# Fourier mix with its features folded a second time, and low parts made in pieces of 256 columns

## The chip, the cores and the metric

The kernel runs on one core of a Trainium2 chip. The time is in device microseconds (us), from the start of the program's execution to its end; lower is better. The engines are PE (matrix products; PEld is its weight loads), DVE, ACT and POOL (elementwise work) and SP (issues most transfers). Each engine executes its own instructions in a fixed order. About 0.3% (2 us) is what a measurement of this kernel can tell from no change.

## The reference

Local and global attention is followed by two mixer blocks on two sequences of 768 tokens with 512 features. The change lies in the second block:

```python
def _moe2_ref(x, w_ch1, w_ch2):
    X = np.fft.fft(x, axis=1)
    X = np.fft.fft(X, axis=2)
    mixed = np.real(X).astype(np.float32)
    u = x + mixed
    mu = np.mean(u, axis=-1, keepdims=True)
    var = np.mean((u - mu) ** 2, axis=-1, keepdims=True)
    un = (u - mu) / np.sqrt(var + 1e-06)
    ch = np.maximum(un @ w_ch1, 0.0) @ w_ch2
    return (u + ch).astype(np.float32)
```

The real part of the two transforms is cos-cos minus sin-sin: tokens times a 768-point table, then features times a 512-point table.

## The kernel before, in words

**Precision.** Products take float32r operands, which keep part of a float32. So each operand is split into a high part (a cast) and a low part (the rest), and a product is three matmuls: high by high, high by low, low by high.

**The main work** is `ffn`: 64 chunks c, each with a word of weights of 128x1024 (512 columns of the first matrix, 512 of the second). Chunk c needs its word c cast to `wh` by ACT (L196), the low part `wo` made by POOL (L200), 12 matmuls of 512 columns (L225; the last four read `wo`), `gh` by ACT (L232) and `gl` by DVE (L233), and 12 matmuls (L248) one chunk later. Chunks 0 to 47 are the first block for three groups of 512 tokens, 48 to 63 the second for one group. The other two groups go through `unit` (L1009, L1059) at the end. Words 0 to 15 are decoded on DVE (L166, L169, L171) as they come in; later ones are read back from a scratch in DRAM.

**The side work** comes in generators that `drive` steps between the main work's steps, at a rate given per stretch of 64 steps: transposes (`tr_gen`), `fft_tables` (loads the cos and sin tables on POOL's DMA queue), `fft(0)`, `norm`, `fft(1)`, `unit_tokens`. Within an engine a scheduler then orders the instructions, so some stand earlier or later than in the code; the rows below headed by an engine show the order that comes out.

**`fft(b)`** for a sequence: `fold` adds and subtracts token tiles, then columns 1 to 255 and 511 to 257 of the features, so the cosine half needs 257 columns and the sine half 255. It makes high and low parts `ee`, `oo` (and `em` for the middle token). First stage: products with tables `c1`, `s1` (L824, L848) give `pt` and `qt`. Second stage: `pcos` (six matmuls L861 of 258 columns, one with `sgn`, L863) and six of 256 columns (L874) for each of three token tiles, and one `pcos` more. ACT and DVE add the results into `x` (L877 to L884).

Of the kernel before, what the change touches and what calls it, by code (L numbers as in the profile page):

```python
# [20 lines left out]
NF = FF // P  # L21
# [3 lines left out]
NL_MAX = 97  # L25
J1 = 386
K1 = 258
JP, KP = 416, 288
KW = S + (NT - 1) * P
PRE_LOAD = (0, 1, 3, 4)  # L30
PRE_DECODE = (2, 3, 4, 6)
# [8 lines left out]
class Prog:  # L40
# [147 lines left out]
    def w_split(self, c):  # L188
        if c >= PLAIN:
            return  # L190
        nc = self.nc
        raw = self.w32.pop(c)
        hi = self.wp.tile([P, 2 * D], FR, tag="whi", bufs=3, name=f"wh{c}")
        lo = self.wp.tile([P, 2 * D], FR, tag="wlo", bufs=3, name=f"wo{c}")
        keep = self.tc.keep_in_program_order if c == 0 else lambda i: i
        keep(nc.scalar.copy(hi, raw))  # L196

        n = 2 * D // (4 if c < NF else 2)
        for z in range(0, 2 * D, n):
            keep(nc.gpsimd.tensor_tensor(lo[:, z:z + n], raw[:, z:z + n], hi[:, z:z + n].bitcast(F32), ALU.subtract))  # L200
        self.wq[c] = (hi, lo)
# [519 lines left out]
    def fft_open(self, ctx):  # L721
        nc, a, tc = self.nc, self.a, self.tc
        self.fp = ctx.enter_context(tc.tile_pool(name="fft", bufs=1))
        fp = self.fp
        self.ct = {}
        shapes = [(f"{n}{z}", shape, w) for n, shape, w in (("c1", [3, JP], J1), ("s1", [3, 384], 384), ("c2", [2, KP], K1),
                                                            ("s2", [2, 256], 256)) for z in range(2)]
        shapes += [("alt", [JP], J1)]

        for n, shape, w in shapes:  # L730
            t = fp.tile([P] + shape, FR, name=n)
            self.ct[n] = t[:, :, 0:w] if len(shape) == 2 else t[:, 0:w]

    def fft_tables(self):
        nc, a, ct = self.nc, self.a, self.ct
        for n in ("c1", "s1", "c2", "s2"):
            for z in range(2):
                nc.gpsimd.dma_start(ct[f"{n}{z}"], a[f"{n}{z}"][:, :, 0:256] if n == "s2" else a[f"{n}{z}"])
                yield
        nc.gpsimd.memset(ct["alt"][64:128, :].bitcast(F32), 0.0)  # L740
        nc.gpsimd.dma_start(ct["alt"][0:64, :], a["alt"])
        yield
        nc.vector.memset(self.mh, -0.5)
# [8 lines left out]
    def fft(self, b):  # L752
        nc, fp, ct = self.nc, self.fp, self.ct
        A = [self.x[b * NT + i] for i in range(3)]
        Bp = [self.x[b * NT + 3 + i] for i in range(3)]
        xm = self.dist[1][:, 0:D]
        nc.gpsimd.memset(xm, 0.0)
        for z in range(2):
            nc.gpsimd.memset(self.dist[z][:, 3 * K1 - 2:3 * K1], 0.0)
        for r in (0, 32):  # L760
            nc.sync.dma_start(xm[r:r + 1, :], Bp[0][0:1, :])
        yield
        ee = fp.tile([P, 2, 3, KP], FR, tag="ee", bufs=1, name=f"ee{b}")[:, :, :, 0:K1]
        oo = fp.tile([P, 2, 3, 256], FR, tag="oo", bufs=1, name=f"oo{b}")
        ee, oo = [ee[:, z] for z in range(2)], [oo[:, z] for z in range(2)]

        def fold(rows, E, O, h, l, i):
            if O is False:
                f = self.qkb[i % 2][:, 1024:1024 + K1]
                nc.vector.tensor_tensor(f[0:rows, 1:256], E[:, 1:256], E[:, 511:256:-1], ALU.add)  # L770
                nc.vector.tensor_copy(f[0:rows, 0:257:256], E[:, 0:257:256])
                nc.vector.memset(f[0:rows, 257:258], 0.0)
            else:
                f = self.vb[i % 2][:, 1024:1024 + K1]
                nc.vector.tensor_tensor(f[0:rows, 1:256], E[:, 1:256], E[:, 511:256:-1], ALU.subtract)
                nc.vector.memset(f[0:rows, 0:1], 0.0)
            n = K1 if O is False else 256
            nc.scalar.copy(h, f[0:rows, 0:n])
            if l is None:
                f, l = f[32:33], h[32:33]  # L780
                nc.vector.tensor_tensor(l, f[:, 0:n], l.bitcast(F32), ALU.subtract)
            else:
                nc.vector.tensor_tensor(l, f[0:rows, 0:n], h.bitcast(F32), ALU.subtract)

        em = fp.tile([P, KP], FR, tag="em", bufs=1, name=f"em{b}")[:, 0:K1]
        for i in range(3):
            E, O = (self.qkb[z][:, (i % 2) * D:(i % 2 + 1) * D] for z in range(2))
            nc.vector.tensor_tensor(E, A[i], Bp[i], ALU.add)
            fold(P, E, False, ee[0][:, i, :], ee[1][:, i, :], i)
            yield  # L790
            nc.vector.tensor_tensor(O, A[i], Bp[i], ALU.subtract)
            fold(P, O, True, oo[0][:, i, :], oo[1][:, i, :], i)
            if i == 1:
                fold(P, xm, False, em, None, 0)
            yield
        if b == 1:
            for _ in range(6):
# [42 lines left out]
        qt = fp.tile([P, 2, 2, 384], FR, tag="ee", bufs=1, name=f"fqt{b}")  # L840
        qt = [qt[:, z] for z in range(2)]
        for dd in range(2):
            cs = slice(dd * P, (dd + 1) * P)
            pp = self.psum("m")
            n = 0
# [6 lines left out]
            h, l = qt[0][:, dd, :], qt[1][:, dd, :]  # L852
# [1 line left out]
            nc.vector.tensor_tensor(l, pp[:, 0:384], h.bitcast(F32), ALU.subtract)  # L854
            yield

        def pcos(out, at):
            n = 0
            for dd in range(2):
                for x, y in PS:  # L860
                    nc.tensor.matmul(out, lhsT=at(pt[x][:, dd, :]), rhs=c2[y][:, dd, :], start=n == 0, stop=False)  # L861
                    n += 1
            nc.tensor.matmul(out, lhsT=at(pr), rhs=ct["sgn"], start=False, stop=True)  # L863

        for i in range(3):
            js = slice(i * P, (i + 1) * P)
            pc = self.psum("m")
            pcos(pc[:, 0:K1], lambda m: m[:, js])
            yield
            qs = self.psum("m2")  # L870
            n = 0
            for dd in range(2):
                for x, y in PS:
                    nc.tensor.matmul(qs[:, 0:256], lhsT=qt[x][:, dd, js], rhs=s2[y][:, dd, :], start=n == 0, stop=n == 5)  # L874
                    n += 1
            qc = self.dist[i % 2][:, 2 * K1:3 * K1]
            nc.scalar.copy(qc[:, 0:256], qs[:, 0:256])  # L877
            sm = self.dist[0][:, 0:K1]
            dm = self.dist[0][:, K1:2 * K1]
            nc.vector.tensor_tensor(dm, pc[:, 0:K1], qc, ALU.subtract)  # L880
            nc.vector.tensor_tensor(sm, pc[:, 0:K1], qc, ALU.add)
            for X, lo_, hi_ in ((A[i], dm, sm), (Bp[i], sm, dm)):
                nc.vector.tensor_tensor(X[:, 0:257], X[:, 0:257], lo_[:, 0:257], ALU.add)
                nc.vector.tensor_tensor(X[:, 511:256:-1], X[:, 511:256:-1], hi_[:, 1:256], ALU.add)  # L884
            yield
        pc = self.psum("m")
        pcos(pc[:, 0:K1], lambda m: same(m[:, 384:385]))
        X = Bp[0]
        nc.vector.tensor_tensor(X[0:1, 0:257], pc[0:1, 0:257], xm[0:1, 0:257], ALU.add)
        nc.vector.tensor_tensor(X[0:1, 511:256:-1], pc[0:1, 1:256], xm[0:1, 511:256:-1], ALU.add)  # L890
        yield

    def norm_one(self, i, z):
# [198 lines left out]


def arm(tc, pg, fast):
# [204 lines left out]
```

## Time and profile before

| | us |
|---|---|
| median of 3 runs | 662.1 |
| runs | 660.75 to 662.32 |
| the profiled execution | 660.77 |
| its span, first to last instruction | 658.4 |
| PE busy | 643.9 |
| DVE busy | 425.1 |
| POOL busy | 344.6 |
| ACT busy | 298.0 |

Busy PE counts overlapping matmuls, so it isn't PE at its peak. How long a matmul really holds PE is the distance from its start to the start of the next one. The mean granted clock of TensorE over the span is 0.995 of full speed.

### The profile page before, as it was taken

The page shows a single profiled execution, that of the slowest core. Times are in us where ns is not written, and L with a number is a line of the kernel's source. Part 1 is how long each engine was busy: PE and PEld are TensorE (multiplying, and loading weights), DVE is VectorE, ACT ScalarE, POOL GpSimd, SP SyncE. Part 2 cuts the span into 40 slices and gives each one's busy share as a digit, 9 for nine tenths or more (in the row PEclk, how much of TensorE's full clock was granted, in tenths as well). Part 3 has the DMA queues.
Part 4 walks back from the last instruction along what each step waited for, and adds up shares of the span by engine and source line. Part 5 has one row for each costly group of instructions (what it writes and reads, how often), then busy time and mean ns, then how long its engine had stood idle before and what let it go on. Part 6 is the DMA issues. An engine that isn't in the chain of part 4 may idle for free.

```text
span 658.4 us, 9572 instructions
## 1 busy us (share of the span) xinstructions
PE 643.9 (98%) x3442; PEld 534.5 (81%) x3442; DVE 425.1 (65%) x784; ACT 298.0 (45%) x584; POOL 344.6 (52%) x360
## 2 busy tenths in 40 slices
PE   7998999999999999999999999999999999999996
PEld 6877777888888888888888888888888888888885
DVE  5889778897839434387467765387556545464544
ACT  5887874554344434335334433334543443233430
POOL 4130235787986554566347665165484664446610
PEclk8999999999999999999999999999999999999998
DMA  7678806888995967666463962112011111011003
GB/s 256 222 275 288 293 35 200 243 246 270 309 335 185 318 216 252 232 199 220 164 208 114 314 226 66 63 65 96 33 67 62 65 64 65 9 56 64 2 2 132
DMA packets 33866, 107.51 MB, mean 163 GB/s; under 512 B 3920, under 2 KB 7952, under 8 KB 30736
## 3 DMA queue, kind: packets, MB, share of 16 engines
q1 hardware_dynamic: 31104, 102.23, 45.8%
q0 software_dynamic: 2416, 3.65, 2.1%
q10 hardware_dynamic: 288, 0.92, 0.4%
q8 instruction: 29, 0.48, 0.3%
q14 instruction: 29, 0.24, 0.1%
HBM read 86.75 MB, written 20.02 MB: 162 GB/s over the span
## 4 chain that ended last, share of the span: by engine, by line
PE 89%; DVE 7%; ACT 2%; issue 1%; DMA 0%; DVEq 0%; ACTq 0%
PE ps_h L225 27%; PE ps_acc L248 27%; PE ps_acc L1059 13%; PE ps_h L1009 10%; DVE p L559 3%; PE ps_sd L1009 2%; DVE pt L591 1%; PE ps_sd L605 1%; PE ps_sd L297 1%; PE ps_sd L824 1%; PE ps_sd L848 1%; PE ps_acc L537 1%; ACT p L571 1%; PE ps_sd L580 1%; PE ps_sd L861 1%
## 5 line engine op out<-in xcount | busy, mean ns | idle before, releaser
L200 POOL TENSOR_TENSOR wo<-w,wh 128x512 fp32r<-128x512 f32 (+1 forms) x160 | 206.6, 1316 | 134.8 <-ACT wh L196 123.4
L225 PE MATMUL ps_h<-uT,wh 128*128 128x512 f32 x512 | 131.5, 393 | 0.0
L196 ACT CAST wh<-w 128x1024 fp32r<-128x1024 f32 x64 | 67.4, 1054 | 101.4 <-PE ps_acc L248 55.5
L225 PEld LDWEIGHTS ps_h<-uT,wh 128*128 128x128 f32 x512 | 94.4, 188 | 19.3 <-issue 0.8
L248 PE MATMUL ps_acc<-wh,gh 128*128 128x512 f32 x256 | 101.0, 395 | 0.0
L248 PE MATMUL ps_acc<-wh,gl 128*128 128x512 f32 x256 | 100.0, 391 | 0.0
L248 PE MATMUL ps_acc<-wo,gh 128*128 128x512 f32 x256 | 99.7, 390 | 0.0
L233 DVE SCALAR_TENSOR_TENSOR gl<-ps_h,gh 128x512 fp32r<-128x512 f32 x64 | 43.8, 684 | 74.0 <-ACT gh L232 74.0
L990 POOL TENSOR_TENSOR uo<-ur,uh 128x256 fp32r<-128x256 f32 (+1 forms) x40 | 42.2, 1065 | 59.6 <-ACT uh L987 59.6
L232 ACT ACTIVATE gh<-ps_h 128x512 fp32r<-128x512 f32 x64 | 38.3, 598 | 70.1 <-PE ps_h L225 70.1
L225 PE MATMUL ps_h<-uT,wo 128*128 128x512 f32 x256 | 69.0, 390 | 0.0
L248 PEld LDWEIGHTS ps_acc<-wh,gl 128*128 128x128 f32 x256 | 48.0, 188 | 10.6 <-DVE gl L233 0.3
L1065 DVE TENSOR_TENSOR xall<-ps_acc,xall 128x512 f32<-128x512 f32 x56 | 38.2, 691 | 28.2 <-PE ps_acc L1059 28.2
L225 PEld LDWEIGHTS ps_h<-uT,wo 128*128 128x128 f32 x256 | 48.0, 188 | 10.3
L248 PEld LDWEIGHTS ps_acc<-wo,gh 128*128 128x128 f32 x256 | 48.1, 188 | 9.6 <-issue 0.2
L248 PEld LDWEIGHTS ps_acc<-wh,gh 128*128 128x128 f32 x256 | 48.1, 188 | 9.4 <-issue 0.2
L571 ACT ACTIVATE p<-p,m 128x256 f32<-128x256 f32 (+2 forms) x96 | 47.6, 499 | 8.7 <-DVE m L559 8.6
L169 DVE SCALAR_TENSOR_TENSOR wr<-wr 128x1024 int32<-128x1024 int32 x30 | 44.1, 1470 | 10.7 <-ACT wr L164 9.5
L987 ACT CAST uh<-ur 128x256 fp32r<-128x256 f32 (+1 forms) x40 | 18.8, 488 | 68.7 <-PE ps_acc L1059 62.9
L1009 PE MATMUL ps_h<-op,uh 128*128 128x512 f32 x160 | 49.3, 389 | 0.0
L559 DVE CUSTOM_DVE_ANT_0 p<-ps_acc,dist 128x256 f32<-128x256 f32 (+2 forms) x96 | 34.9, 419 | 7.4 <-PE ps_acc L542 6.8
L1009 PEld LDWEIGHTS ps_h<-op,uh 128*128 128x128 f32 x160 | 30.0, 188 | 6.3
(268 smaller groups left out, 1142.6 us busy)
## 6 DMA issues: line engine op xcount, KB each, us to landing
w<-wscr SPq DMA_DIRECT2D x48, 512.0 KB, 4.2
wr<-wl SPq DMA_DIRECT2D x17, 1024.0 KB, 7.8
wr<-wl SPq DMA_DIRECT2D x60, 256.0 KB, 5.4
wscr<-w SPq DMA_DIRECT2D x16, 512.0 KB, 8.4
wscr<-wd SPq DMA_DIRECT2D x16, 512.0 KB, 3.0
ur<-wscr SPq DMA_DIRECT2D x16, 512.0 KB, 4.5
qk<-qkg SPq DMA_DIRECT2D x7, 1088.0 KB, 7.7
vb<-vw SPq DMA_DIRECT2D x7, 768.0 KB, 5.1
```

The costliest lines, as they stand in the source:

```text
L169: pin(nc.vector.scalar_tensor_tensor(lo, hi, 3, lo, ALU.logical_shift_left, ALU.bitwise_or))
L196: keep(nc.scalar.copy(hi, raw))
L200: keep(nc.gpsimd.tensor_tensor(lo[:, z:z + n], raw[:, z:z + n], hi[:, z:z + n].bitcast(F32), ALU.subtract))
L225: nc.tensor.matmul(hp, lhsT=w[:, dd * P:(dd + 1) * P], rhs=u[:, dd, :], start=n == 0, stop=n == 11)
L232: nc.scalar.activation(gh, hp, AF.Relu)
L233: nc.vector.scalar_tensor_tensor(gl, hp, 0.0, gh.bitcast(F32), ALU.max, ALU.subtract)
L248: nc.tensor.matmul(acc[t], lhsT=g[:, s], rhs=w[:, D:2 * D], start=pf == 0 and m == 0, stop=pf == NF - 1 and m == 2)
L559: keep(nc.vector.tensor_tensor_reduce(out=T[z][:, s], in0=sp[z][:, s], in1=self.dist[z][:, dcol[t]:dcol[t] + width[t]], op0=ALU.add, op1=A ...
L571: keep(nc.scalar.activation(T[z][:, s], T[z][:, s], AF.Exp, bias=m[:, z, y:y + 1], scale=-1.0, accum_out=sm[:, u % 2, y, z:z + 1]))
L990: nc.gpsimd.tensor_tensor(lo[:, s], src, hi[:, s].bitcast(F32), ALU.subtract)
L1009: keep(nc.tensor.matmul(out, lhsT=x[:, s], rhs=y[:, kt, :], start=start and kt + n == 0, stop=kt + n == 3, skip_group_check=not start))
L1059: keep(nc.tensor.matmul(acc[t], lhsT=x[:, s], rhs=y[:, w], start=first and n == 0, stop=not first and n == 2))
```

## The change

It does four things. The folded features are folded once more (128 and 129 columns), which parts the second stage's outputs into even and odd columns: each product then has the first or the second half of the contraction and 130 columns, where both halves had 258 or 256. The tables `c2` and `s2` are therefore loaded raw (`c2r`, `s2r`) and every second column of them is copied by ACT into the tables in use. Results are interleaved again as they are read. `w_split` makes `wo` in four pieces of 256 columns for all words; before, words 16 to 63 had two of 512. The last stretch's side rate goes from 1.33 to 1.42.

```diff
@@ w_split
-        n = 2 * D // (4 if c < NF else 2)
+        n = 2 * D // 4
@@ fft_tables
+        for n in ("c2", "s2"):
+            raw = []
+            for z in range(2):
+                r, src, row = self.fp.tile([P, KP], FR, tag=f"r{z}", bufs=1, name=f"{n}r{z}")[:, 0:K1], a[f"{n}{z}"], int(n == "s2")
+                raw.append(r)
+                nc.gpsimd.dma_start(r[row:P, :], src[row:P, 0, :])
+                if row:
+                    nc.gpsimd.dma_start(r[0:1, :], src[0:1, 1, :])
+            yield
+            for z in range(2):
+                t, r = ct[f"{n}{z}"], raw[z]
+                nc.vector.memset(t[:, :, KH - 1:KH].bitcast(F32), 0.0)
+                for y in range(2):
+                    nc.scalar.copy(t[:, y, 0:KH - 1], r[:, y:K1:2])
                 yield
@@ fold
             if O is False:
-                f = self.qkb[i % 2][:, 1024:1024 + K1]
-                nc.vector.tensor_tensor(f[0:rows, 1:256], E[:, 1:256], E[:, 511:256:-1], ALU.add)
-                nc.vector.tensor_copy(f[0:rows, 0:257:256], E[:, 0:257:256])
-                nc.vector.memset(f[0:rows, 257:258], 0.0)
+                f, g = (self.qkb[i % 2][0:rows, o:o + 257] for o in (1024, 1312))
+                nc.vector.tensor_tensor(f[:, 1:256], E[0:rows, 1:256], E[0:rows, 511:256:-1], ALU.add)
+                nc.scalar.copy(f[:, 0:257:256], E[0:rows, 0:257:256])
+                nc.vector.tensor_tensor(g[:, 0:128], f[:, 0:128], f[:, 256:128:-1], ALU.add)
+                nc.vector.tensor_tensor(g[:, 128:256], f[:, 0:128], f[:, 256:128:-1], ALU.subtract)
+                nc.scalar.copy(g[:, 256:257], f[:, 128:129])
             else:
...
+                nc.vector.tensor_tensor(g[:, 0:128], f[:, 0:128], f[:, 256:128:-1], ALU.subtract)
+                nc.vector.tensor_tensor(g[:, 128:256], f[:, 0:128], f[:, 256:128:-1], ALU.add)
+                nc.scalar.copy(g[:, 128:129], f[:, 128:129])
@@ second stage
-        def pcos(out, at):
-            n = 0
-            for dd in range(2):
-                for x, y in PS:
-                    nc.tensor.matmul(out, lhsT=at(pt[x][:, dd, :]), rhs=c2[y][:, dd, :], start=n == 0, stop=False)
-                    n += 1
-            nc.tensor.matmul(out, lhsT=at(pr), rhs=ct["sgn"], start=False, stop=True)
+        def pcos(pc, at):
+            for t, out in enumerate(halves(pc)):
+                for n, (x, y) in enumerate(PS):
+                    nc.tensor.matmul(out, lhsT=at(pt[x][:, t, :]), rhs=c2[y][:, t, :], start=n == 0, stop=t == 1 and n == 2)
+                if t == 0:
+                    nc.tensor.matmul(out, lhsT=at(pr), rhs=ct["sgn"][:, 0:KH], start=False, stop=True)
...
@@ arm
-                              pg.unit_tokens()), 1.33)
+                              pg.unit_tokens()), 1.42)
```

**ACT at the table loads.** Names carry their word or chunk: `wh16` is the high part of word 16, `gh15` the output of chunk 15; `c2r0` is the raw cosine table, `DMASW` a transfer on POOL's queue. Before, ACT's order there is:

```order
L196 CAST wh15_2115<-w15_2080 128x1024 [waits DVE_49,PE_49]
L232 ACTIVATE gh14_2137<-ps_h_2124 128x512 [waits PE_49,Activation_49]
L196 CAST wh16_2153<-w16_2122 128x1024 [waits DMAHW0_49,PE_49,Pool_49]
L232 ACTIVATE gh15_2173<-ps_h_2160 128x512 [waits DVE_49,PE_49]
L196 CAST wh17_2203<-w17_2158 128x1024 [waits DMAHW2_49,PE_49,Pool_49]
L232 ACTIVATE gh16_2226<-ps_h_2212 128x512 [waits DVE_49,PE_49]
```

and now:

```order
L232 ACTIVATE gh14_2137<-ps_h_2124 128x512 [waits PE_49,Activation_49]
L754 COPY c20_2200<-c2r0_2589 128x129 [waits DMASW4_49]
L754 COPY c20_2200<-c2r0_2589 128x129
L754 COPY c21_2201<-c2r1_2591 128x129 [waits DMASW5_49]
L196 CAST wh16_2153<-w16_2122 128x1024 [waits DMAHW0_49,PE_49,Pool_49]
L754 COPY c21_2201<-c2r1_2591 128x129
L232 ACTIVATE gh15_2175<-ps_h_2162 128x512 [waits DVE_49,PE_49]
L754 COPY s20_2202<-s2r0_2711 128x129 [waits DMASW2_49,DMASW1_49]
L754 COPY s20_2202<-s2r0_2711 128x129
L754 COPY s21_2203<-s2r1_2714 128x129 [waits DMASW4_49,DMASW3_49]
L196 CAST wh17_2205<-w17_2160 128x1024 [waits DMAHW2_49,PE_49,Pool_49]
```

The casts of words 16 and 17 now stand behind copies that wait for the tables' transfers.

**POOL at the same place** issues those transfers; before:

```order
L200 TENSOR_TENSOR wo_2116<-w_2080,wh_2115 128x256 x3
L738 DMA c_2198<-c 128x2x258
L738 DMA c_2199<-c 128x2x258
L738 DMA s_2200<-s 128x2x256
L738 DMA s_2201<-s 128x2x256
L740 MEMSET alt 64x386 [waits Pool_49]
L741 DMA alt<-alt 64x386 [waits DMASW0_49]
L200 TENSOR_TENSOR wo_2154<-w_2122,wh_2153 128x512 [waits DMAHW0_49,Activation_49,Pool_49]
```

and now (`wo_2116` is word 15's, `wo_2154` word 16's):

```order
L200 TENSOR_TENSOR wo_2116<-w_2080,wh_2115 128x256 x3
L746 DMA c2r_2589<-c 128x258
L746 DMA c2r_2591<-c 128x258
L756 MEMSET alt 64x386 [waits Pool_49]
L757 DMA alt<-alt 64x386
L766 DMA sgn<-sgn 64x258
L766 DMA sgn<-sgn 64x258 [waits DMASW0_49]
L746 DMA s2r_2711<-s 127x258 [waits DMASW4_49,DMASW1_49,Activation_49]
L748 DMA s2r_2711<-s 1x6x43 [waits DMASW2_49]
L832 CAST sp_3214<-em_3052 128x2x32 [waits Pool_49]
L200 TENSOR_TENSOR wo_2154<-w_2122,wh_2153 128x256 [waits DMAHW0_49,Activation_49]
L746 DMA s2r_2714<-s 127x258 [waits DMASW5_49,DMASW3_49,Activation_49]
```

The second raw sine table is requested only behind word 16's low part, and the first only when ACT has copied the cosine table out of its tile.

**DVE in the last token tile's fold of `fft(1)`.** Before:

```order
L788 TENSOR_TENSOR qk0_67<-xall1_186 128x512
L783 TENSOR_TENSOR ee1_3883<-qk1_68,ee1_3883 128x258
L783 TENSOR_TENSOR oo1_3884<-vb1_72,oo1_3884 128x256
L781 TENSOR_TENSOR em1_3885<-qk0_67,em1_3885 1x258
L791 TENSOR_TENSOR qk1_68<-xall1_186 128x512
L770 TENSOR_TENSOR qk0_67<-qk0_67 128x255
L771 COPY qk0_67<-qk0_67 128x2
L772 MEMSET qk0_67 128x1
L775 TENSOR_TENSOR vb0_71<-qk1_68 128x255
L776 MEMSET vb0_71 128x1
L233 SCALAR_TENSOR_TENSOR gl50_3985<-ps_h_3971,gh50_3984 128x512
L783 TENSOR_TENSOR ee1_3883<-qk0_67,ee1_3883 128x258
```

and now:

```order
L807 TENSOR_TENSOR qk0_67<-xall1_186 128x512
L802 TENSOR_TENSOR em1_4002<-qk0_67,em1_4002 1x257
L786 TENSOR_TENSOR qk0_67<-qk0_67 128x255
L810 TENSOR_TENSOR qk1_68<-xall1_186 128x512
L788 TENSOR_TENSOR qk0_67<-qk0_67 128x128
L789 TENSOR_TENSOR qk0_67<-qk0_67 128x128
L793 TENSOR_TENSOR qk0_67<-qk1_68 128x255
L794 MEMSET qk0_67 128x2
L233 SCALAR_TENSOR_TENSOR gl50_4108<-ps_h_4094,gh50_4107 128x512
L802 TENSOR_TENSOR ee1_4000<-qk0_67,ee1_4000 128x257
```

The last low part of `ee` closes this fold as it did. From the first fold instruction of `fft(1)` to it there are now twelve additions of 128 columns more, and the four small copies (L771) are gone to ACT.

## Rows read from the trace of the kernel before

**Rows 1.** The page, busy time of engines and shares of the chain.

```profile
PE 643.9 (98%) x3442; PEld 534.5 (81%) x3442; DVE 425.1 (65%) x784; ACT 298.0 (45%) x584; POOL 344.6 (52%) x360
...
PE 89%; DVE 7%; ACT 2%; issue 1%; DMA 0%; DVEq 0%; ACTq 0%
```

**Rows 2.** Timeline of PE: start, length, line, tiles, count; second stage of `fft(0)`.

```profile
330.31 0.87 PE L861 MATMUL ps_sd<-c,fpt 128*128 128x258 f32 x6
331.01 0.28 PE L863 MATMUL ps_sd<-sgn,fpr 128*128 128x258 f32 x1
331.13 1.54 PE L225 MATMUL ps_h<-uT,wh 128*128 128x512 f32 x6
332.51 0.89 PE L874 MATMUL ps_sd<-s,fqt 128*128 128x256 f32 x6
333.24 0.63 PE L225 MATMUL ps_h<-uT,wh 128*128 128x512 f32 x2
```

**Rows 3.** Timelines of PEld after a wait, and of PE's narrowest run.

```profile
95.79 0.19 PEld L225 LDWEIGHTS ps_h<-uT,wh 128*128 128x128 f32 x1 [0.31 <-DVE uT L300]
...
95.90 0.19 PEld L225 LDWEIGHTS ps_h<-uT,wh 128*128 128x128 f32 x1
...
27.01 1.97 PE L605 MATMUL ps_sd<-pt,vb 128*64 128x128 f32 x32
```

**Rows 4.** Timeline of POOL at the table loads.

```profile
181.81 2.82 POOL L200 TENSOR_TENSOR wo<-w,wh 128x256 fp32r<-128x256 f32 x4 [1.25 <-ACT wh L196]
184.58 1.46 POOL L738 DMA_DIRECT2D c<-c  x2
```

**Rows 5.** DMA issues in single windows there: size, median us to landing.

```profile
s<-s POOLq DMA_DIRECT2D x2, 576.0 KB, 9.3
...
c<-c POOLq DMA_DIRECT2D x2, 258.0 KB, 7.7
...
dist<-xall SPq DMA_DIRECT2D x2, 2.0 KB, 4.0
```

**Rows 6.** Timeline of ACT there, with idle time and what ended it.

```profile
184.37 1.05 ACT L196 CAST wh<-w 128x1024 fp32r<-128x1024 f32 x1 [2.15 <-DMA w<-wscr]
...
190.76 1.05 ACT L196 CAST wh<-w 128x1024 fp32r<-128x1024 f32 x1 [3.34 <-DMA w<-wscr]
```

**Rows 7.** Timeline of PE there: first matmuls of chunks 16 and 17.

```profile
189.34 1.98 PE L225 MATMUL ps_h<-uT,wh 128*128 128x512 f32 x8
...
195.13 2.09 PE L225 MATMUL ps_h<-uT,wh 128*128 128x512 f32 x8
```

**Rows 8.** Timeline of DVE, then POOL, during the fold of `fft(1)`.

```profile
388.02 0.68 DVE L788 TENSOR_TENSOR qk<-xall 128x512 f32<-128x512 f32 x1
...
391.83 0.41 DVE L775 TENSOR_TENSOR vb<-qk 128x255 f32<-128x255 f32 x1
...
401.67 0.41 DVE L783 TENSOR_TENSOR ee<-qk,ee 128x258 fp32r<-128x258 f32 x1
...
388.29 3.27 POOL L200 TENSOR_TENSOR wo<-w,wh 128x512 fp32r<-128x512 f32 x2 [2.91 <-ACT wh L196]
```

**Rows 9.** Timeline of PE at the matmuls that need this fold.

```profile
401.43 1.14 PE L824 MATMUL ps_sd<-c,ee 128*128 128x386 f32 x4
402.41 0.34 PE L828 MATMUL ps_sd<-alt,em 128*128 128x386 f32 x1
```

**Rows 10.** POOL's low part of word 44, and PE's first use of it.

```profile
358.13 2.66 POOL L200 TENSOR_TENSOR wo<-w,wh 128x512 fp32r<-128x512 f32 x2
...
360.52 1.09 PE L225 MATMUL ps_h<-uT,wo 128*128 128x512 f32 x4
```

**Rows 11.** Windows: us, busy us (count) PE, PEld, DVE, ACT, POOL, clock, DMA share.

```profile
10.00:15.00 5.00, 1.99 (x12) 1.61 (x12) 3.09 (x17) 4.71 (x17) 2.09 (x7) 0.80 0.79 290
15.00:20.00 5.00, 5.00 (x39) 4.34 (x38) 4.34 (x18) 3.10 (x12) 0.83 (x1) 0.86 0.65 267
...
13.01 1.66 PE L537 MATMUL ps_acc<-qk 64*128 64x128 f32 x8 [3.06 <-DVE m L559]
```

More of the change, by code (lines that the diff above doesn't have):

```diff
@@ L27 @@
 K1 = 258
-JP, KP = 416, 288
+JP, KP, KH = 416, 288, 130
 KW = S + (NT - 1) * P
@@ L725, in fft_open @@
         self.ct = {}
-        shapes = [(f"{n}{z}", shape, w) for n, shape, w in (("c1", [3, JP], J1), ("s1", [3, 384], 384), ("c2", [2, KP], K1),
-                                                            ("s2", [2, 256], 256)) for z in range(2)]
+        shapes = [(f"{n}{z}", shape, w) for n, shape, w in (("c1", [3, JP], J1), ("s1", [3, 384], 384)) for z in range(2)]
+        shapes += [(f"{n}{z}", [2, KH], KH) for n in ("c2", "s2") for z in range(2)]
         shapes += [("alt", [JP], J1)]
@@ L735, in fft_tables @@
         nc, a, ct = self.nc, self.a, self.ct
-        for n in ("c1", "s1", "c2", "s2"):
+        for n in ("c1", "s1"):
             for z in range(2):
-                nc.gpsimd.dma_start(ct[f"{n}{z}"], a[f"{n}{z}"][:, :, 0:256] if n == "s2" else a[f"{n}{z}"])
+                nc.gpsimd.dma_start(ct[f"{n}{z}"], a[f"{n}{z}"])
+                yield
[7 more added lines that the diff above has]
+                    nc.gpsimd.dma_start(r[0:1, :], src[0:1, 1, :])
+            yield
+            for z in range(2):
[3 more added lines that the diff above has]
+                    nc.scalar.copy(t[:, y, 0:KH - 1], r[:, y:K1:2])
                 yield
@@ L757, in fft @@
         nc.gpsimd.memset(xm, 0.0)
-        for z in range(2):
-            nc.gpsimd.memset(self.dist[z][:, 3 * K1 - 2:3 * K1], 0.0)
         for r in (0, 32):
@@ L768, in fold @@
             if O is False:
-                f = self.qkb[i % 2][:, 1024:1024 + K1]
-                nc.vector.tensor_tensor(f[0:rows, 1:256], E[:, 1:256], E[:, 511:256:-1], ALU.add)
-                nc.vector.tensor_copy(f[0:rows, 0:257:256], E[:, 0:257:256])
-                nc.vector.memset(f[0:rows, 257:258], 0.0)
-            else:
[L774 to L778, printed above, removed]
+                f, g = (self.qkb[i % 2][0:rows, o:o + 257] for o in (1024, 1312))
[4 more added lines that the diff above has]
+                nc.scalar.copy(g[:, 256:257], f[:, 128:129])
+            else:
+                f, g = self.qkb[i % 2][0:rows, 1600:1857], self.vb[i % 2][0:rows, 1024:1280]
+                nc.vector.tensor_tensor(f[:, 1:256], E[0:rows, 1:256], E[0:rows, 511:256:-1], ALU.subtract)
+                nc.vector.memset(f[:, 0:257:256], 0.0)
+                nc.vector.tensor_tensor(g[:, 0:128], f[:, 0:128], f[:, 256:128:-1], ALU.subtract)
+                nc.vector.tensor_tensor(g[:, 128:256], f[:, 0:128], f[:, 256:128:-1], ALU.add)
+                nc.scalar.copy(g[:, 128:129], f[:, 128:129])
+            nc.scalar.copy(h, g)
             if l is None:
[L780 to L783, printed above, removed]
+                g, h = g[32:33], h[32:33]
+                l = h
+            nc.vector.tensor_tensor(l, g, h.bitcast(F32), ALU.subtract)
         em = fp.tile([P, KP], FR, tag="em", bufs=1, name=f"em{b}")[:, 0:K1]
@@ L788, in fft @@
             nc.vector.tensor_tensor(E, A[i], Bp[i], ALU.add)
-            fold(P, E, False, ee[0][:, i, :], ee[1][:, i, :], i)
+            fold(P, E, False, ee[0][:, i, 0:257], ee[1][:, i, 0:257], i)
             yield
@@ L793, in fft @@
             if i == 1:
-                fold(P, xm, False, em, None, 0)
+                fold(P, xm, False, em[:, 0:257], None, 0)
+                nc.vector.memset(em[:, 257:258].bitcast(F32), 0.0)
             yield
@@ L855, in fft, with halves, both, inter @@
             yield
-        def pcos(out, at):
-            n = 0
-            for dd in range(2):
-                for x, y in PS:
-                    nc.tensor.matmul(out, lhsT=at(pt[x][:, dd, :]), rhs=c2[y][:, dd, :], start=n == 0, stop=False)
-                    n += 1
-            nc.tensor.matmul(out, lhsT=at(pr), rhs=ct["sgn"], start=False, stop=True)
+        def halves(pc):
+            return [pc[:, y * 256:y * 256 + KH] for y in range(2)]
+        def pcos(pc, at):
[4 more added lines that the diff above has]
+                    nc.tensor.matmul(out, lhsT=at(pr), rhs=ct["sgn"][:, 0:KH], start=False, stop=True)
+        def both(pc):
+            return pc.rearrange("p (t k) -> p t k", t=2)[:, :, 0:KH]
+        def inter(v):
+            return v.rearrange("p (k t) -> p t k", t=2)
+        sm, dm = (self.dist[0][:, z * 2 * KH:(z + 1) * 2 * KH] for z in range(2))
         for i in range(3):
@@ L867, in fft @@
             pc = self.psum("m")
-            pcos(pc[:, 0:K1], lambda m: m[:, js])
+            pcos(pc, lambda m: m[:, js])
             yield
             qs = self.psum("m2")
[L871 to L881, printed above, removed]
+            for t, out in enumerate(halves(qs)):
+                for n, (x, y) in enumerate(PS):
+                    nc.tensor.matmul(out, lhsT=qt[x][:, t, js], rhs=s2[y][:, t, :], start=n == 0, stop=n == 2)
+            qc = self.dist[i % 2][:, 4 * KH:6 * KH].rearrange("p (t k) -> p t k", t=2)
+            nc.scalar.copy(qc, both(qs))
+            nc.vector.tensor_tensor(inter(dm), both(pc), qc, ALU.subtract)
+            nc.vector.tensor_tensor(inter(sm), both(pc), qc, ALU.add)
             for X, lo_, hi_ in ((A[i], dm, sm), (Bp[i], sm, dm)):
@@ L886, in fft @@
         pc = self.psum("m")
-        pcos(pc[:, 0:K1], lambda m: same(m[:, 384:385]))
+        pcos(pc, lambda m: same(m[:, 384:385]))
+        nc.scalar.copy(inter(sm[0:1]), both(pc[0:1]))
         X = Bp[0]
-        nc.vector.tensor_tensor(X[0:1, 0:257], pc[0:1, 0:257], xm[0:1, 0:257], ALU.add)
-        nc.vector.tensor_tensor(X[0:1, 511:256:-1], pc[0:1, 1:256], xm[0:1, 511:256:-1], ALU.add)
+        nc.vector.tensor_tensor(X[0:1, 0:257], sm[0:1, 0:257], xm[0:1, 0:257], ALU.add)
+        nc.vector.tensor_tensor(X[0:1, 511:256:-1], sm[0:1, 1:256], xm[0:1, 511:256:-1], ALU.add)
         yield
```

## The prediction

> **What bounds the kernel now.** I read the page first, for the busy shares and the chain. PE is busy 98% of the span and carries 89% of the chain; DVE, the next engine, is busy 65% [rows 1]. So an edit counts where it changes how long a matmul holds PE, or where it makes PE wait for something it did not wait for before; work taken from or given to DVE, ACT or POOL is free as long as PE's operands are still there in time. Then I went to the timelines of the four places that the diff touches: the second stage on PE [rows 2], the table loads on POOL and ACT with the matmuls that depend on them [rows 4 to 7], the fold on DVE with its reader on PE [rows 8, 9], and a low part made with little to spare [rows 10]. At the last three the reader should compare two times, when the operand is ready and when PE asks for it: the cover is their difference.
>
> The sum is made on the profiled execution, 660.8 us, which lies 1.3 us under the median of 662.1.
>
> **The second stage's matmuls.** Each product has half the contraction at about half the width, so the count stays: 7 in each of four `pcos` per sequence, 56 for both, and 6 for each of three tiles, 36 for both. What changes is the width, 258 or 256 to 130. Before, seven `pcos` matmuls hold PE from 330.31 to 331.13, 117 ns each, and six sine ones from 332.51 to 333.24, 122 ns each [rows 2]. How fast 130 columns go with 128 columns of weights no row shows in such a stretch. Each still has its own weight load, and two loads right behind each other start 0.11 us apart, at 95.79 and 95.90 [rows 3]. From that I take 112 ns: 56 x 5 + 36 x 10 = 0.6 us, say 0.7 saved. The bounds: the narrow matmuls of 128 columns with weights of 64 columns took 1.97 us for 32, 62 ns each [rows 3], which would save 56 x 55 + 36 x 60 = 5.2 us; weights half as wide make that the far end. On the other side, no row shows float32r operands under 256 columns wide, so nothing excludes that they run slower; I bound them by the matmul of 512 columns, 230 ns (331.13 to 332.51 for six [rows 2]), with which 92 x 112 = 10.3 us would be lost. I stay at the weight load, since 128 columns of weights are loaded in both versions, and it is the row with the same shape.
>
> The Trainium skill, "TensorE: Matmul & The Clock Gate", section "Back-to-back issue gap", speaks against my small figure: it gives about 81 ns for each pair of load and matmul at 128 columns in a sustained stream. By an estimate from it the stage would save 92 x (119 - 81) = 3.5 us. The same sentence gives 131 ns at 512 columns, where the trace has the 230 ns named above; the measurement decides, so I give the rule little weight.
>
> **The tables `c2` and `s2`.** This is the main term. Before, four transfers went straight into the tables, and nothing but the second stage, far later, waited for them. Now ACT copies out of the raw tiles, and in ACT's order the casts of words 16 and 17 stand behind copies that wait for those transfers. PE asks for the first cast at 189.34 and for the second at 195.13 [rows 7]; before, the casts began at 184.37 and 190.76 and took 1.05 us [rows 6], so each had 3 to 4 us of cover. That is less than a transfer takes.
>
> First wait. POOL issues the cosine tables at 184.58, two in 1.46 us [rows 4], right behind word 15's low part, as before. Then they took a median of 7.7 us to land with 258 KB for two [rows 5], the sine tables of the first stage being ahead of them in the queue. With half the bytes I take 192.2 for the second one, between 184.6 + 4.0 + the issue (190) and before's 185.3 + 7.7 (193). A copy of 129 columns should take some 0.2 us (the cast of 1024 took 1.05), so the cast of word 16 ends at 192.2 + 0.2 + 1.05 = 193.5, and PE, which asks at 189.3, stands still for 4.1 us (2 to 5).
>
> Second wait. POOL's order puts word 16's low part between the two sine tables. It can start when the cast ends, takes four pieces of 0.70 (2.82 for four [rows 4]), and only then, at 196.3, is the second sine table requested. From issue to landing the rows have 4.0 us for small transfers, 7.7 for the cosine tables and 9.3 for a full sine table [rows 5]. I take the middle of 4.0 and 7.7, since by then little stands ahead in the queue: landed at 202.2. With the copy and the cast of word 17, which stands behind it on ACT, 203.4. PE wanted it at 195.13: 8.3 us late. The first wait lies inside this figure (both delay the same stream), so the pair costs 8.3, not 12.4. The ends: 4.0 us give 6.4, 9.3 give 11.7. Behind the waiting copies on ACT are also `gh15` and `gh16`, which PE wants later than the casts, so they add nothing.
>
> **The fold of `fft(1)`.** DVE works through it without a break from 388.02 to the last low part of `ee`, 401.67 + 0.41 = 402.08 [rows 8]. PE is just there: its four matmuls that need `ee` start at 401.43 and the next at 402.41 [rows 9], so there is no cover, and what DVE takes longer PE waits. The change adds twelve additions of 128 columns. An addition of 512 took 0.68 and one of 255 took 0.41 [rows 8], so 0.27 for half; from these 128 columns cost 0.20 to 0.28, together 2.4 to 3.4. The four copies gone to ACT give back some 0.3. POOL's low parts in this stretch, two pieces in 3.27 [rows 8], become four. Whether DVE and POOL slow one another more so is open; I add 0.2. Taken: 2.9 - 0.3 + 0.2 = 2.8, less a little for a new order of the additions: 2.7, with ends of 0 (if PE has got something else to do ahead of these matmuls) and 4.3. PE has as many instructions ahead of this place as before, although the rate is 1.42: the later side work moves earlier by some matmuls, and I cost that at nothing, since its operands come from work that stands earlier too. The fold of `fft(0)` is about even.
>
> **Low parts in pieces of 256.** Four pieces cost 2.82, two cost 2.66 [rows 4, 10]. The tightest word that I found is 44: its first half is ready after half of 2.66, at 359.46, and PE's four matmuls that read it start at 360.52 [rows 10], 1.06 us later. Two pieces of four take 1.41, which leaves 0.98. I take 0.3 for places where this is not enough (0 to 1).
>
> **The clock.** After a wait of 3.06 us that ended at 13.01, the granted clock is 0.80 in one window and 0.86 in the next [rows 11]. That is (0.20 + 0.14) x 5 / 0.5 = 3.4 us at 1.2 GHz, the lower of the two levels, in which 1.7 us of work are lost. A PE wait of 4 us is as long. What the first loses lies inside the second's wait; the second may cost up to 1.7, and a third, at the fold, another 1.7. The fold's wait is under 3.06 us. Taken: 0.5 (0 to 3.4).
>
> **The sum.** 660.8 + 8.3 + 2.7 - 0.7 + 0.3 + 0.5 = 671.9 us.
>
> **The rivals.** First, tables that hold nobody up: if the transfers land before 189 the casts are not late. For it: half the bytes, and DMA queues that are mostly idle. Against it: it needs under 3 us for both, and no transfer in the rows has that. Then only the fold stays: 660.8 + 2.7 - 0.7 + 0.3 = 663.1, within 0.3%. Second, the other side, faster: narrow matmuls at the far end of 62 ns, together with tables in time. That gives 660.8 - 5.2 + 2.7 + 0.3 = 658.6, and 655.9 if the fold costs nothing as well; it decides only if the waits at the tables cost PE under 1.5 us (under 4.2 with the fold free), and against it are the 128 columns of weights and the cover of 3 to 4 us. With the page's 81 ns in place of 62 it would be 1.7 more. Third, the second table comes at the far end, 9.3 us or more, and the clock drops behind both waits: 660.8 + 11.7 + 4.3 - 0.7 + 1 + 3.4 = 680.5. Fourth, narrow matmuls as slow as 512 columns: 671.9 + 0.7 + 10.3 = 682.9. Nothing in the rows speaks for it, nothing excludes it.
>
> **How the numbers follow.** Forecast (both table waits, longer fold) 0.72; third rival 0.08; fourth 0.06; the first 0.08; the faster one 0.06. A measurement of this kernel can tell about 0.3% (2 us) from no change. Only the second rival is faster by that, and half of the first may stray to either side: faster 0.06, within 0.3% 0.07, slower 0.87. The forecast's own terms at their near ends give 660.8 + 6.4 + 0 - 0.7 - 1.5 (half of what narrower matmuls could bring beyond that, rounded down) = 665.0, which is the range's low end. The high end is 680, the third rival: 0.86 of the chance is to lie between.
>
> **What would show it.** In the profile after: ACT's copies at L754 idle before them, ended by a transfer of `c2r` or `s2r`; idle time of PE before the first L225 matmuls of chunks 16 and 17, some 4 us at 189 and another 4 near 199; PE waiting on the last low part of `ee` from DVE 2 to 3 us longer; six-matmul groups of the second stage 0.67 us apart. The forecast is wrong if ACT's copies find their tables landed, if PE's groups of the second stage take 0.4 us or 1.4 us, or if PE's wait lies at a place not named here.

## The result, and the profile after

The changed kernel takes 669.9 us (median of 4 runs, 667.4 to 671.3), the kernel before 661.4 in the same comparison: a ratio of 1.0125, 95% interval 1.0088 to 1.0162. The forecast was 671.9, within 665 to 680. The profiled execution after took 670.4 us with a span of 668.6, 10.2 more than the span before.

On the page PE is busy about as long as before [rows 1], 648.1 us against 643.9, but its share of the chain fell from 89% to 67%:

```profile
PE 648.1 (97%) x3442; PEld 537.0 (80%) x3442; DVE 428.8 (64%) x802; ACT 303.6 (45%) x616; POOL 371.3 (56%) x454
...
PE 67%; DVE 6%; ACT 2%; DMA 1%; issue 1%; POOL 0%; DVEq 0%; ACTq 0%
```

The first place is the table loads. This is PE's timeline (start, length, line, tiles, count, idle time before and what ended it), which answers to [rows 7]:

```profile
187.97 0.39 PE L248 MATMUL ps_acc<-wh,gl 128*128 128x512 f32 x1
193.92 3.78 PE L225 MATMUL ps_h<-uT,wh 128*128 128x512 f32 x8 [5.57 <-ACT wh L196]
197.50 1.91 PE L225 MATMUL ps_h<-uT,wo 128*128 128x512 f32 x4
199.20 0.63 PE L248 MATMUL ps_acc<-wh,gh 128*128 128x512 f32 x1
...
202.73 2.09 PE L225 MATMUL ps_h<-uT,wh 128*128 128x512 f32 x8
```

ACT's timeline there, against [rows 6]:

```profile
191.67 0.51 ACT L754 CAST c<-c2r 128x129 fp32r<-128x129 f32 x2 [10.57 <-DMA c2r<-c]
192.62 0.31 ACT L754 CAST c<-c2r 128x129 fp32r<-128x129 f32 x1 [0.44 <-DMA c2r<-c]
192.83 1.04 ACT L196 CAST wh<-w 128x1024 fp32r<-128x1024 f32 x1
...
200.65 0.51 ACT L754 CAST s<-s2r 128x129 fp32r<-128x129 f32 x2 [2.84 <-DMA s2r<-s]
201.06 1.05 ACT L196 CAST wh<-w 128x1024 fp32r<-128x1024 f32 x1
```

And POOL's, against [rows 4]:

```profile
183.47 1.10 POOL L746 DMA_DIRECT2D c2r<-c  x2
...
192.48 0.57 POOL L746 DMA_DIRECT2D s2r<-s  x1 [5.94 <-ACT c L754]
...
193.95 2.79 POOL L200 TENSOR_TENSOR wo<-w,wh 128x256 fp32r<-128x256 f32 x4
196.70 0.58 POOL L746 DMA_DIRECT2D s2r<-s  x1
```

ACT stands still for 10.57 us until the cosine table has landed; the cast of word 16, whose word had landed at 185.6, ends at 193.87, and PE, which asked at 188.2, starts chunk 16 at 193.92. The second sine table is requested behind word 16's low part, lands at 200.6, and word 17's cast ends at 202.1. Chunk 17 starts at 202.73. Before it started at 195.13 [rows 7], and this execution had come to the place 1.15 us earlier than the one before (by the starts of the same main matmuls on both sides, from 112 us on). So the place costs 202.73 - (195.13 - 1.15) = 8.75 us. The windows show the clock (core time, busy us and count of PE, PEld, DVE, ACT, POOL, then granted clock, DMA share, GB/s):

```profile
190.00:195.00 5.00, 1.08 (x3) 0.90 (x4) 0.40 (x1) 2.46 (x6) 2.35 (x5) 0.83 1.04 289
195.00:200.00 5.00, 5.00 (x13) 3.95 (x12) 0.29 (x1) 0.52 (x2) 2.78 (x5) 0.50 0.46 146
```

0.50 is 1.2 GHz. From 193.9 to 200.1 fourteen matmuls of 512 columns take 6.1 us, some 0.43 us each in place of 0.23: 3 us lost. With the wait before them, 5.7 us by the starts, that makes the place's cost.

The second place is the fold of `fft(1)`. DVE, against [rows 8], first and last operation and two of the new additions:

```profile
395.08 0.68 DVE L807 TENSOR_TENSOR qk<-xall 128x512 f32<-128x512 f32 x1
...
404.76 0.82 DVE L788 TENSOR_TENSOR qk<-qk 128x128 f32<-128x128 f32 x1
405.51 0.28 DVE L789 TENSOR_TENSOR qk<-qk 128x128 f32<-128x128 f32 x1
...
411.11 0.42 DVE L802 TENSOR_TENSOR ee<-qk,ee 128x257 fp32r<-128x257 f32 x1
```

PE, against [rows 9]:

```profile
408.47 0.34 PE L844 MATMUL ps_sd<-c,ee 128*128 128x386 f32 x1
410.79 0.62 PE L844 MATMUL ps_sd<-c,ee 128*128 128x386 f32 x2 [1.98 <-ACT ee L798]
411.58 0.59 PE L844 MATMUL ps_sd<-c,ee 128*128 128x386 f32 x1 [0.17 <-DVE ee L802]
411.96 0.53 PE L848 MATMUL ps_sd<-alt,em 128*128 128x386 f32 x1
412.29 0.63 PE L248 MATMUL ps_acc<-wh,gh 128*128 128x512 f32 x1
```

The window there:

```profile
410.00:415.00 5.00, 4.04 (x11) 3.14 (x12) 4.24 (x11) 2.20 (x6) 3.72 (x6) 0.67 0.07 13
```

The fold takes DVE 16.45 us, where it took 14.06: 2.4 longer. From the first of PE's four matmuls to the next main one there are 3.82 us, before 1.16 (401.43 to 402.59): 2.66 more. The long part of PE's wait, 1.98, is for the high part of `ee`, which ACT casts at 410.34, its last addition on DVE having ended at 410.24; only 0.17 is for the low part. The six main matmuls behind them run at the lower clock as well (0.67 granted in the window), 1.2 us lost. By the starts of the same main matmuls on both sides the place costs 4.0.

The third is the second stage, against [rows 2]:

```profile
337.74 0.45 PE L884 MATMUL ps_sd<-c,fpt 128*128 128x130 f32 x3
338.02 0.27 PE L886 MATMUL ps_sd<-sgn,fpr 128*128 128x130 f32 x1
338.14 0.50 PE L884 MATMUL ps_sd<-c,fpt 128*128 128x130 f32 x3
338.47 1.60 PE L225 MATMUL ps_h<-uT,wh 128*128 128x512 f32 x6
339.90 0.78 PE L903 MATMUL ps_sd<-s,fqt 128*128 128x130 f32 x6
340.52 0.68 PE L225 MATMUL ps_h<-uT,wh 128*128 128x512 f32 x2
```

The three matmuls from 338.14 take 0.33 us, 0.11 each. The three from 337.74 take 0.28: the first behind a matmul of 512 columns holds PE for only 0.06. In PEld's records the second's load starts together with the first matmul, at 337.74, and the second matmul 0.06 behind its load, as the later ones do; their loads start 0.11 apart. Summed over all 92, by the distance of starts, the stage takes 9.6 us where it took 11.1: 1.5 saved.

The three places and the early start make the span's difference: 8.75 + 4.0 - 1.5 - 1.15 = 10.1, of 10.2.

### The profile page after: what moved, and what is told of

It reads as the page before. It is cut to its first block, busy times and chain, and to the rows that moved or that the text cites. A ratio compares the mean times of both kernels' runs of the same rounds, so it can differ in the third digit from the quotient of the medians.

```text
span 668.6 us, 9725 instructions
## 1 busy us (share of the span) xinstructions
PE 648.1 (97%) x3442; PEld 537.0 (80%) x3442; DVE 428.8 (64%) x802; ACT 303.6 (45%) x616; POOL 371.3 (56%) x454
## 4 chain that ended last, share of the span: by engine, by line
PE 67%; DVE 6%; ACT 2%; DMA 1%; issue 1%; POOL 0%; DVEq 0%; ACTq 0%
PE ps_acc L248 19%; PE ps_h L225 19%; PE ps_acc L1086 13%; PE ps_h L1036 10%; DVE wr L169 2%; PE ps_sd L1036 2%; DVE w L171 2%; DMA c2r<-c 1%; ACT wh L196 1%; PE ps_sd L868 1%; ACT wr L164 1%; PE ps_sd L844 1%; PE ps_sd L297 1%; PE ps_sd L884 1%; PE ps_sd L903 1%
## 5 line engine op out<-in xcount | busy, mean ns | idle before, releaser
L200 POOL TENSOR_TENSOR wo<-w,wh 128x256 fp32r<-128x256 f32 x256 | 236.4, 954 | 117.9 <-ACT wh L196 100.9
L225 PEld LDWEIGHTS ps_h<-uT,wh 128*128 128x128 f32 x512 | 95.8, 190 | 26.2 <-ACT wh L196 6.2
L248 PE MATMUL ps_acc<-wh,gh 128*128 128x512 f32 x256 | 102.5, 400 | 0.0
L169 DVE SCALAR_TENSOR_TENSOR wr<-wr 128x1024 int32<-128x1024 int32 x30 | 45.6, 1519 | 11.2 <-ACT wr L164 10.4
```

Source lines behind the costliest of these rows:

```text
L169: pin(nc.vector.scalar_tensor_tensor(lo, hi, 3, lo, ALU.logical_shift_left, ALU.bitwise_or))
L225: nc.tensor.matmul(hp, lhsT=w[:, dd * P:(dd + 1) * P], rhs=u[:, dd, :], start=n == 0, stop=n == 11)
L248: nc.tensor.matmul(acc[t], lhsT=g[:, s], rhs=w[:, D:2 * D], start=pf == 0 and m == 0, stop=pf == NF - 1 and m == 2)
```

## The experiments

Times of the kernel before, run beside each, are 660.6 us for the first four runs and 661.0 for the last four. Of each, the ratio to it is what counts.

**A raw tile for each table**, so that the second table's lateness goes and the first wait stays:

```diff
-        for n in ("c2", "s2"):
-            raw = []
+        raw = {}
+        for n in ("c2", "s2"):
             for z in range(2):
-                r, src, row = self.fp.tile([P, KP], FR, tag=f"r{z}", bufs=1, name=f"{n}r{z}")[:, 0:K1], a[f"{n}{z}"], int(n == "s2")
-                raw.append(r)
+                r, src, row = self.fp.tile([P, 264], FR, tag=f"{n}r{z}", bufs=1, name=f"{n}r{z}")[:, 0:K1], a[f"{n}{z}"], int(n == "s2")
+                raw[n, z] = r
...
+        for n in ("c2", "s2"):
             for z in range(2):
-                t, r = ct[f"{n}{z}"], raw[z]
+                t, r = ct[f"{n}{z}"], raw[n, z]
...
```

> The changed kernel with a raw tile of its own for each of the four tables, so that both sine tables are requested right behind the cosine tables instead of behind ACT's copies and word 16's low part. The copies stand on ACT where they stood. In the changed kernel PE waits 5.7 us at chunk 16, then runs 14 matmuls at the lower clock (0.20 us extra each, 3.0 us in all) and reaches chunk 17 at 202.7, while the cast of word 17 has ended at 202.1. Theory A (the late second sine table sets the loss, as forecast): without it PE keeps only the first wait, 3 us faster, about 667. Theory B (the first wait and the clock that it costs set the loss, the second table's lateness lies beside them): at most 0.6 us faster, about 669.5, and PE's wait at chunk 16 is again 5 to 6 us.

668.6 us, ratio 1.0126 (1.0094 to 1.0157): by this the same as the changed kernel. PE and ACT:

```profile
195.54 3.60 PE L225 MATMUL ps_h<-uT,wh 128*128 128x512 f32 x8 [5.65 <-ACT wh L196]
198.98 1.08 PE L225 MATMUL ps_h<-uT,wo 128*128 128x512 f32 x4
...
202.97 2.09 PE L225 MATMUL ps_h<-uT,wh 128*128 128x512 f32 x8
```

```profile
195.60 0.93 ACT L755 CAST s<-s2r 128x129 fp32r<-128x129 f32 x4
...
196.92 1.04 ACT L196 CAST wh<-w 128x1024 fp32r<-128x1024 f32 x1
```

Word 17's cast now ends at 197.96, five us before PE asks for it; and yet PE loses 7.4 us (5.8 of wait, then seven matmuls at the lower clock, 1.6). That is 1.4 less than in the changed kernel's trace, where the clock stayed low for twice as many. By the ratio theory B is met and theory A is not, but each interval reaches some 2 us to either side, so the times alone don't exclude A's 3 us. The trace speaks for B: with word 17's cast early, the first wait and the clock behind it still make up 7.4 of 8.75 us, and in the changed kernel the second table comes late beside them.

**Copies held back**, ahead of the first stage of `fft(0)`:

```diff
@@ fft, ahead of the first stage
+        if b == 0:
+            for n in ("c2", "s2"):
+                for z in range(2):
+                    t, r = ct[f"{n}{z}"], raw[n, z]
...
+                        self.tc.keep_in_program_order(nc.scalar.copy(t[:, y, 0:KH - 1], r[:, y:K1:2]))
+                    yield
```

> The changed kernel with four raw tiles and with ACT's copies and the loads of sgn held back in program order, between the fold and the first stage of the first sequence, some 100 us after the transfers landed. Nothing else differs. Theory (the copies' place in ACT's order costs 8.7 us): the wait at chunk 16 is gone and the granted clock stays at 1.00 there; 669.9 - 8.7 = 661.2. Rival (half of it comes from elsewhere, such as low parts that stand behind POOL's transfers): 664 to 667 and a wait of PE that remains between 185 and 205.

664.6 us, ratio 1.0054 (1.0034 to 1.0074). The four raw tiles of the last run stay, and the loads of `sgn` are held in program order too. PE has no wait from 115 us to 305; the raw tiles alone had left it, so the wait at the tables hangs on the copies' place. But the time stayed 3.4 above what was expected, within the rival's 664 to 667, though not for the rival's reason: no wait is left between 185 and 205. The held copies moved the first stage behind the next main work, and that brought a wait at another place:

```profile
305.47 0.50 PE L248 MATMUL ps_acc<-wh,gl 128*128 128x512 f32 x1 [1.59 <-DVE gl L233]
```

In the changed kernel the first stage's matmuls run while DVE finishes that `gl`. At the fold of `fft(1)` PE waited as in the changed kernel (2.5 us for ACT's casts of `ee`). Whether these two are all of the 3.4 the trace doesn't settle.

**More main work between the fold and its reader** (the edit of the last run stays):

```diff
-            for _ in range(6):
+            for _ in range(10):
                 yield
```

> As the run before, and in the second sequence ten steps instead of six lie between the fold and its first reader on PE, so that PE does 18 more of the main matmuls (4.1 us) before it asks. Theory (the longer fold costs its wait of 2.15 us and 2.0 us at the lower clock behind it, together 4.2): 661.2 - 4.2 = 657.0, faster than the kernel before by some 0.6%. Rival (only the wait itself comes back, or the later side work is then late for the tail): 659 to 661.

666.0 us, ratio 1.0083 (1.0060 to 1.0107): nothing gained, neither by the theory's number nor by the rival's. PE's reader of `ee` comes late enough now and doesn't wait, but another does:

```profile
405.19 0.50 PE L248 MATMUL ps_acc<-wh,gl 128*128 128x512 f32 x1 [3.00 <-DVE gl L233]
```

DVE shows why: the `gl` of that chunk, whose input was there at 401.4, stands behind the fold.

```profile
401.56 0.68 DVE L802 TENSOR_TENSOR qk<-xall 128x512 f32<-128x512 f32 x1
...
404.12 0.41 DVE L788 TENSOR_TENSOR qk<-qk 128x255 f32<-128x255 f32 x1
404.46 0.68 DVE L233 SCALAR_TENSOR_TENSOR gl<-ps_h,gh 128x512 fp32r<-128x512 f32 x1
```

From the start of the `gl` before it, at 393.69, to this one DVE takes 10.8 us, most of it fold; the kernel before has 7.6 there (393.48 to 401.06). My theory on the fold was too narrow here: it isn't only its reader that waits for it.

**The wait alone, in the kernel before:**

```diff
@@ fft_tables of the kernel before, behind the loads of c2
+            if n == "c2":
+                dump = self.fp.tile([P, 2, 2], FR, tag="dump", bufs=1, name="dump")
+                for z in range(2):
+                    nc.scalar.copy(dump[:, z, :], ct[f"c2{z}"][:, 0, 0:2])
+                yield
```

> The kernel before with one thing of the change: ACT copies two columns of each cosine table of the second stage into a spare tile, right behind the loads; nobody reads them. In ACT's order the first copy stands ahead of the cast of word 16 and waits for the transfer, which landed at 192.1 when PE asked for the cast at 189.3. Theory (an ACT wait for a transfer delays the cast, PE stands 4 us and the clock then costs 3 more): 661.4 + 7 = 668.4. Rival (the wait alone counts): 661.4 + 4 = 665.4. If transfers are no cause: 661.4.

666.1 us, ratio 1.0082 (1.0060 to 1.0104), 5.5 us more for two copies of two columns.

```profile
191.63 0.19 ACT L743 CAST dump<-c 128x2 fp32r<-128x2 f32 x1 [9.11 <-DMA c<-c]
191.73 1.04 ACT L196 CAST wh<-w 128x1024 fp32r<-128x1024 f32 x1
```

```profile
192.82 3.40 PE L225 MATMUL ps_h<-uT,wh 128*128 128x512 f32 x8 [3.02 <-ACT wh L196]
196.02 1.40 PE L225 MATMUL ps_h<-uT,wo 128*128 128x512 f32 x4
```

The mechanism stands by itself: 3.2 us of wait and 1.7 at the lower clock (3.40 for eight matmuls that take 1.98 in [rows 7]). The 5.5 us lie between the theory's 7 and the rival's 4. The wait is shorter than the expected 4 since the transfer landed 6.7 us after its issue, at 191.6; why the clock stayed low for a shorter time is not shown.

**Copies held back to just ahead of the second stage.** As the second run, with the copies behind the first stage and without steps of their own.

> The changed kernel with four raw tiles and ACT's copies held back to just before the second stage of the first sequence, so that PE's and DVE's order at that sequence's first stage is again that of the changed kernel (in the run with the copies ahead of the first stage it was not, and PE waited 1.75 us at 305 for a low part `gl`). Theory: no wait of PE from 180 to 205 nor at 305; what is left against the kernel before is the fold's wait with its slower clock (4.2) less the narrower second stage (1.5): +2.7, 663.4 against 660.6. Rival (the held copies cost by their new place, in front of word casts on ACT): 665 or more.

662.3 us, ratio 1.0023 (1.0008 to 1.0039): 1.1 under the theory's number, and the rival's 665 is not met. No wait from 115 to 402 us; what is left is the fold, in PE's timeline the same as in the changed kernel:

```profile
402.48 0.62 PE L839 MATMUL ps_sd<-c,ee 128*128 128x386 f32 x2 [1.96 <-ACT ee L793]
403.26 0.45 PE L839 MATMUL ps_sd<-c,ee 128*128 128x386 f32 x1 [0.17 <-DVE ee L797]
```

**The fold spread.** On top of the last run:

```diff
@@ fft, fold loop: after each half of a token tile
-            yield
+            for _ in range(3 if b == 1 else 1):
+                yield
@@ behind the loop
-            for _ in range(6):
+            for _ in range(0):
                 yield
```

> As the run before, with the six steps that followed the second sequence's fold put between its parts (three steps in place of one after each half of a token tile), so that DVE's low parts `gl` stand between 2.2, 4.9 and 3.6 us of fold, in place of one behind 7.1 (sums of the operations' own durations). Theory (the fold costs because DVE does it in one piece, and whoever stands behind it waits, its reader on PE or the next `gl`): the wait goes, 660.6 - 1.5 = 659.1, no slower than before. Rival (the fold's own length costs, wherever it stands): 662 to 663.4.

659.1 us, ratio 0.9974 (0.9960 to 0.9988): 1.9 us under the kernel before, with an interval clear of 1 but no more than the 2 us that such a measurement can tell, and 3.2 under the run without the spread. The additions are all there; what PE still waits is

```profile
401.13 0.50 PE L248 MATMUL ps_acc<-wh,gl 128*128 128x512 f32 x1 [0.15 <-DVE gl L233]
...
407.24 0.86 PE L841 MATMUL ps_sd<-c,ee 128*128 128x386 f32 x4
```

and the granted clock stays at 1.00. So the fold's length costs next to nothing by itself here; its standing in one piece on DVE does.

**Pieces of 512 again**, on the run with the copies at their use:

```diff
-        n = 2 * D // 4
+        n = 2 * D // (4 if c < NF else 2)
```

> The run with the copies at their use, with low parts of words 16 to 63 in two pieces of 512 as before the change. Theory (pieces cost at most 0.3 us): 663.4, within 0.5 of that run, and the fold's wait on PE as long as there. Rival (four pieces disturb DVE's fold more than two): 1 us or more faster, with a shorter fold.

663.0 us, ratio 1.0032 (1.0013 to 1.0051), against 1.0023 with four pieces. No difference that the intervals show, and PE waits as long at the fold, 2.3 us against 2.1. POOL's busy time for low parts is 208.8 us in place of 230.9, and none of it shows in the time.

**The side rate of 1.33 again**, on the same run:

```diff
-                              pg.unit_tokens()), 1.42)
+                              pg.unit_tokens()), 1.33)
```

> The run with the copies at their use, with the last stretch's side rate 1.33 as before the change. Theory (the rate moves only side work behind the fold, costed at nothing): 663.4, within 0.5 of that run. Rival (the faster rate crowds the fold or the tail): 1 us or more faster with 1.33.

662.6 us, ratio 1.0026 (1.0013 to 1.0039): the same again.

## Why the prediction was right

**The tables, 8.3 forecast, 8.75 in the trace.** The step held: casts behind copies that wait for transfers, a second transfer that is requested only behind word 16's low part. The parts were sized differently. The first wait was 5.7, not 4.1 (over the stated 5), since PE came to the place earlier against transfers that landed no earlier: half the bytes took 8.2 and 8.6 us, where the full tables took a median of 7.7 [rows 5]. The first rival leaned on DMA queues that are mostly idle; here the DMA engines were full from 180 to 195 (shares of 1.04 to 1.19). The second wait, some 4 us at 199, did not show: PE ran at the lower clock until 200.1 and reached chunk 17 when its cast had just ended. The forecast took its 8.3 from the second table: word 17's cast late at 203.4. In the trace it ended at 202.1, some 8.1 after PE would have wanted it, but PE was held as long by something else, 5.7 of first wait and 3.0 at the lower clock. That the two paths end within 0.6 us of each other is luck, and so is part of the agreement. As the prediction says, what the first wait's clock loses lies inside the second; but the first run shows that it works the other way round as well: without the second table's lateness PE still lost 7.4. That the copies' place is the cause is shown by taking it away (no wait) and by putting such a wait alone into the kernel before (5.5 us more). By the runs the place costs less than in the trace: the ratio falls from 1.0125 to 1.0023 with the copies at their use, 6.7 us, give or take 2.7.

**The fold, 2.7 forecast.** Measured 2.4 more on DVE and 2.66 more on PE. Twelve additions at 0.20 us each, as their starts are apart where POOL leaves DVE alone, give 2.4. The four copies gone to ACT give back 0.3, and POOL takes 0.35 more: eight operations of this fold stand beside a low part and are 0.55 longer each, 4.4 in all, where before it were four and 4.0. So the forecast's -0.3 and 0.2 were near too. PE waited mostly for the high part of `ee`, where the prediction had named the low part; both stand behind the same additions.

**The clock, 0.5 forecast, 1.2 to 1.5 at the fold.** This term was too small. I let the lower clock follow only a wait of 3 us or more [rows 11] and passed the fold over because its wait is shorter; a wait of 1.98 us was followed by the same fall. At the tables the clock lost 3.0, where 1.7 was forecast, inside the second wait.

**The second stage, 0.7 forecast, 1.5 saved.** The distance within a group is 0.11 us, as taken from the weight loads in [rows 3]; that the load sets it is argued from the equal distances, no run changed it. The step left out that the first matmul of a group, behind a wide one, costs only half of that: thirteen such places make most of the missing 0.8. The 81 ns of the Trainium skill ("TensorE: Matmul & The Clock Gate", section "Back-to-back issue gap") are not reached here: the mean over the stage is 104.

**Pieces and rate, 0.3 and nothing forecast.** Neither moves the time beyond the intervals.

The sum came out 2 us high against the median of 669.9: it adds 11.1 to the execution profiled before, where the medians lie 8.5 apart. The profiled executions lie 9.6 apart, of which the start of 1.15 us less is no part of the change; in them the misses in the second stage and the clock have opposite signs and cancel, which is luck.

The runs after spread from 667.4 to 671.3. Their mean granted clock is 0.994 in the fastest and 0.989 to 0.990 in the three others; over 668 us that is about 3 us of work at full speed, as much as the fastest is ahead on average. So the spread goes with the clock. At which places it fell in the executions without a trace is not shown.

## What to carry to other kernels

Where an engine executes in order, a small copy that waits for a transfer costs what stands behind it, not what it takes itself: look at what follows it in that engine's order, and hold such copies back to where they are used. Work that is spread thinly over a long run can be free, and the same work in one piece not: before the reader is moved, look for who else stands behind it. Here, with the copies already held back, the spreading took the change from 0.2% slower to 0.3% faster.

## What the runs showed of the hardware

The fall of TensorE's granted clock is not told by the length of the wait alone. It followed waits of 1.98 us (the changed kernel at its fold, 0.67 granted from 410 to 415), 1.96 (the run with the copies at their use, 0.72 from 405 to 410) and 3.02 (the kernel before with the wait, 0.83 in both windows from 190 to 200), but in the profiled execution of the run with ten steps a wait of 3.00 us that ended at 405.19 was followed by none. That execution, 663.6 us with a mean clock of 0.998, was the fastest of its runs; the others, up to 667.4, have 0.989 to 0.994.

```profile
400.00:405.00 5.00, 2.19 (x9) 1.19 (x7) 4.94 (x15) 3.43 (x10) 1.53 (x4) 1.00 0.31 105
405.00:410.00 5.00, 4.81 (x22) 4.13 (x23) 3.08 (x6) 2.03 (x4) 4.04 (x8) 1.00 0.26 88
```

The transfers' time from issue to landing did not follow their size. The half cosine tables took 8.2 to 8.6 us in the changed kernel, with the DMA engines full (a share of 1.19 in the window from 185 and 1.04 from 190), where the full ones took a median of 7.7 before; over the runs that request the half tables at this place it was 6.0 to 8.7. The half sine tables, as large, took 3.7 to 4.6 us a few us later, while the share fell to 0.46. Which part the engines' load has in this, and which the transfers ahead in the same queue, no run separates.

The same addition of 128 columns takes DVE 0.28 us alone and 0.82 beside a low part of 256 columns on POOL (404.76 and 405.51 above). Beside one of 512 it took 1.37 to 1.39, three times in the run with pieces of 512. So each of four pieces lengthened a DVE operation by 0.55 and each of two by up to 1.10, which is why their number made no difference to DVE here.
